# Causal attention feeding a soft mixture of experts: joining chunk maxima with two one-operand VectorE reductions on a gapped row, and routing products ahead of attention's value products

## Chip, cores and metric

One Trainium2 chip, one core. The metric is the device time of one execution in microseconds (us), and lower is better. The kernel before has a median of 550.02 us over three runs (547.91 to 552.44).

## What is computed

The reference, cut to what matters:

```python
def _attn_ref(q, k, v):                       # (8, 12, 448, 64) each, float32
    scores = scale * np.matmul(q, k.transpose(0, 1, 3, 2))
    scores = np.where(mask, -1000000000.0, scores)          # causal
    scores = scores - np.max(scores, axis=-1, keepdims=True)
    attn = np.exp(scores)
    attn = attn / (np.sum(attn, axis=-1, keepdims=True) + 1e-09)
    return np.matmul(attn, v)

def _moe_ref(x, phi, w1, w2):                 # x: (3584, 768), phi: (768, 32)
    logits = x @ phi
    d = softmax of logits over the 3584 tokens, per slot
    slot_out = 8 experts on d.T @ x           # 4 slots each, 768 -> 1024 -> 768, relu
    c = softmax of logits over the 32 slots, per token
    return c @ slot_out
```

Attention over 8 batches of 12 heads gives `x`, the input of a soft mixture of experts: every one of the 32 slots is a weighted sum of all tokens, goes through its expert, and is handed back to all tokens with other weights.

## The kernel before, in words

The engines are named as the profile does: PE (TensorE, with PEld for its weight loads), DVE (VectorE), ACT (ScalarE), POOL (GpSimd) and SP (SyncE, which issues the loads). Every operation is issued through a helper class that keeps each engine's instructions in the order in which the program writes them. So all instructions carry one line, L70, and groups are told apart by their tiles.

**The loop.** The 96 heads are taken one after the other (line 511), two heads to a pair that shares its loads. Twelve heads make a batch of the experts' part. One pass of the loop, number i, works on several heads at once, and the table `ORDER` (lines 48 to 53, one row for even passes and one for odd) says in which order it issues the steps:

- `c0`, `c3`, `c12`, `k0` to `k3`: the causal mask and the scores of head i+2 on PE, into tile `s`, 1024 columns of PSUM. Keys lie on the partitions in four chunks of 128, and chunk c has the columns of the queries that it may serve: 448, 320, 192 and 64 columns.
- `x0` to `x3` (`max_keys`, line 277): the largest score of each query block of head i+2, on DVE. `x0` is one transposing reduction of `s` into a row `r` of 32 numbers, one for each 32 columns of `s`. Since a query block lies in up to four chunks, `x1` to `x3` join the chunks: three `tensor_tensor` maxima, in place in `r`, of 10, 6 and 2 numbers.
- `mr0`, `mr1` (`max_row`): for head i+1, a PE transpose of 14 columns of `r` into `rt`, and a DVE reduction of it into `mr`.
- `sp` (`max_spread`): POOL spreads `mr` over the queries, into `r2`, for head i+1.
- `t0` to `t3` (`scores2`): PE adds the low-order parts of the operands and the maximum to the scores of head i.
- `exp`: ACT writes the exponentials of head i from `s` to `pt`.
- `a0` to `a3` (`attv`): PE multiplies `pt` of head i-1 with the values, 64 small products into `po`; `n0` to `n2` (`norm`): DVE adds epsilon to the sums (`sm`), takes the reciprocal, and writes the normalised head to `x`.
- `ck`, `cq`, `c2` on ACT (casts and copies of loaded keys and queries) and `sk`, `sq` on POOL (`tensor_tensor` subtractions, 64 x 896, that leave the low-order parts `ks` and `r2`): one of each for a pair.
- `pa` and `plan`: the experts' part. `pa` is a transpose of a finished pair (`xt` on PE, copied to `xts` by ACT), in passes 0, 1, 3, 5, 9 and 10 of each twelve, or a transpose of the weights (`tp`), in pass 4. `plan` is the products with the routing matrix (`g` on PE, added to `lt` by DVE; passes 2, 8 and 11, with two more small DVE steps, `bm` and `run_m`, in pass 2), or the slots' weighted sums (`sp` on PE, added to `si` by DVE; passes 6 and 7). Before the change `plan` is the last step of a pass, so on PE it stands behind the 64 value products and on DVE behind `n2`.

**Buffers that tie the engines.** `s` has three buffers. `rt`, `xt`, `tp`, `g` and the slots' sums share a single PSUM buffer (`misc`, line 210), so each of them waits until DVE or ACT has read the one before. `po` is single.

**After the loop** the expert weights that did not fit (23 of the tiles are loaded during the loop) stream in, the experts run on PE, and the result is written.

Of the kernel before, what the change touches and what calls it, by code (L numbers as in the profile page):

```python
# [9 lines left out]
F32 = mybir.dt.float32  # L10
# [3 lines left out]
ALU = mybir.AluOpType  # L14
AX = mybir.AxisListType
PSUM = bass.MemoryType.PSUM

P = 128
# [3 lines left out]
AW = 32  # L22
# [4 lines left out]
NQB = S // 32  # L27
# [4 lines left out]
NHD = 2 * NPAIR  # L32
# [14 lines left out]

ORDER = (
# [4 lines left out]
)  # L53

SC0, SC1, SC2, SC3 = 512, 0, 320, 960
CQ0 = (0, 128, 256, 384)
SCOL = (SC0, SC1, SC2, SC3)

# [27 lines left out]
def attention_soft_moe(ctx: ExitStack, tc: tile.TileContext, qk, va, phi, w1, w2, out):  # L86
    nc = _Core(tc)
# [7 lines left out]
    wk = early.enter_context(tc.tile_pool(name="wk", bufs=1, side="right"))  # L95
    fix = early.enter_context(tc.tile_pool(name="fix", bufs=1, side="right"))
# [6 lines left out]
    x_, va_, pt_ = [None] * XB, [None, None], [None, None]  # L103
    qd_, ks_ = ([fix.tile([P, 2, S], F32R, name=f"{o}0")] for o in ("qd", "ks"))
    x_[1] = fix.tile([P, NCH, 3 * P], F32, name="x1")
    qd_.append(fix.tile([P, 2, S], F32R, name="qd1"))
    zero = fix.tile([P, P // 2], F32, name="zero")
    ks_.append(fix.tile([P, 2, S], F32R, name="ks1"))
    r2_ = [fix.tile([P, 2, S], F32R, name="r20")]
    va_[0] = fix.tile([P, NCH, 2, VC], F32, name="va0")  # L110

    k2_ = fix.tile([P, 2, S], F32R, name="k2")
    r2_.append(fix.tile([P, 2, S], F32R, name="r21"))
    pt_[0] = wk.tile([P, 1025], F32, name="pt0")
    va_[1] = wk.tile([P, NCH, 2, VC], F32, name="va1")
    pt_[1] = wk.tile([P, 1025], F32, name="pt1")
    lt = moe.tile([P, P], F32, name="lt")

    x_[2] = moe.tile([P, NCH, 3 * P], F32, name="x2")
# [4 lines left out]
    st = {}  # L124
# [63 lines left out]
    ident = const.tile([P, P], F32, name="ident")  # L188
# [16 lines left out]
            nc.vector.memset(k2_[0:64, :, :].bitcast(F32), 1.0)  # L205
    nc.vector.memset(po0, 0.0)
    for i in range(2):
        nc.vector.memset(pt_[i][:, 1024:1025], 0.0)

    def misc(name):  # L210
        return ps_1.tile([P, 512], F32, tag="m", name=name)
# [64 lines left out]

    def max_keys(i, k):

        if i >= NHD:
            return  # L280
        if k == 0:
            r = st["r", i] = wk.tile([P, 32], F32, tag="r", name=f"r{i}", bufs=2)
            nc.vector.tensor_reduce(out=r, in_=st["s", i].rearrange("p (b k)->p b k", k=32),
                                    axis=AX.X, op=ALU.max, apply_transpose=True)
        else:
            r, c0, c, q = st["r", i], SC0 // 32, SCOL[k] // 32, CQ0[k] // 32
            rq = r[:, c0 + q:c0 + NQB]
            nc.vector.tensor_tensor(out=rq, in0=rq, in1=r[:, c:c + NQB - q], op=ALU.max)

    def max_row(i, k):  # L290
        if i >= NHD:
            return
        if k == 0:
            st["rt", i] = misc(f"rt{i}")
            nc.tensor.transpose(out=st["rt", i][0:NQB, 0:P], in_=st.pop(("r", i))[:, SC0 // 32:SC0 // 32 + NQB], identity=ident)
        else:
            mr = st["mr", i] = wk.tile([NQB, 32], F32, tag="mr", name=f"mr{i}", bufs=2)
            nc.vector.tensor_reduce(out=mr, in_=st.pop(("rt", i))[0:NQB, 0:P].rearrange("p (g t)->p t g", g=4),
                                    axis=AX.X, op=ALU.max, negate=True)

    def max_spread(i):
        if i >= NHD:
            return
        p, h = divmod(i, 2)
        mr = st.pop(("mr", i))

        nc.gpsimd.affine_select(out=r2_[p % NR][0:NQB, h].rearrange("p (b t)->p b t", t=32),
                                in_=mr.unsqueeze(1).to_broadcast([NQB, NQB, 32]),
                                compare_op=ALU.is_equal, fill=0.0, base=0,
                                pattern=[[-1, NQB], [0, 32]], channel_multiplier=1)  # L310
# [16 lines left out]
    def attv(i, qcs):  # L327
        if not 0 <= i < NHD:
            return
        p, h = divmod(i, 2)  # L330
        pt, v, po = pt_[i % 2], va_[p % 2], st.get(("po", i), po0)
        begun = st.setdefault(("begun", i, id(po)), set())
        for qc in qcs:
            for c in range(qc + 1):
                col = SCOL[c] + P * (qc - c)
                for u in range(0, P if qc < 3 or i == NHD - 1 and c < 3 else 64, AW):
                    nc.tensor.matmul(po[u:u + AW, qc], pt[:, col + u:col + u + AW], v[:, c, h],
                                     start=u not in begun, stop=c == qc, skip_group_check=True)
                    begun.add(u)
# [43 lines left out]
    def logits_b(b, l):  # L383
        bm = st["bm", b] = moe.tile([P, 1], F32, tag="bm", name=f"bm{b}", bufs=2)
        nc.vector.tensor_reduce(out=bm, in_=l, axis=AX.X, op=ALU.max, negate=True)

        mo, mn = run_m[(b + 1) % 2], run_m[b % 2]
        nc.vector.tensor_tensor(out=mn, in0=mo, in1=st.pop(("bm", b)), op=ALU.min)

    def logits_d(b, l):  # L390
        mo, mn = run_m[(b + 1) % 2], run_m[b % 2]
# [42 lines left out]
    plan, plan_a = {}, {}  # L434
    for b in range(NB):
        o, last = 12 * b, b == NB - 1
        for j, r in enumerate((3, 5, 9, 10, 12, 13)):
            if not last or j < PPB - 2:
                plan_a[o + r] = lambda p=b * PPB + j: xtrans(p)
        for j, r in ((0, 8), (2, 11)):  # L440
            plan[o + r] = lambda b=b, j=j: next_logits(b, j, misc(f"g{b}_{j}"))
        if not last:
            plan[o + 14] = lambda b=b: (next_logits(b, 4, misc(f"g{b}_4")), logits_b(b, lt))
            plan_a[o + 16] = lambda b=b: logits_e(b)
            plan[o + 18] = lambda b=b: dispatch(b, 0)
            plan[o + 19] = lambda b=b: dispatch(b, 1)
# [21 lines left out]
    copy_k2(0, h1)  # L468
    cast_q(1, h1)

    for i, k in ((0, 0), (0, 1), (0, 2), (0, 3), (1, 0)):
        max_keys(i, k)
    sub_k(1, h0)
    max_row(0, 0)
    warm(START[5], po0.rearrange("p a b->p (a b)")[:, 0:2 * P])
    scores1_all(2)
    warm(START[3])
    max_row(0, 1)
    max_spread(0)
    for k in (1, 2, 3):  # L480
        max_keys(1, k)
    sub_q(1, h0)

# [27 lines left out]
    for i in range(NHD):  # L511
        p, h = divmod(i, 2)
# [11 lines left out]
        if i < 2:  # L524
            scores2(i, (1, 0, 2))
            if i:
                scores1_all(3)
            scores2(i, (3,))
            exps(i)
            if i == 0:  # L530
                max_row(1, 0)
                warm(START[4], po0.rearrange("p a b->p (a b)")[:, 0:P])
                max_row(1, 1)
                sub_k(1, h1, nc.vector)
                max_spread(1)
                sub_q(1, h1)
# [37 lines left out]
    i, b, p = NHD - 1, NB - 1, NPAIR - 1  # L574
# [3 lines left out]
    mo, mn = run_m[(b + 1) % 2], run_m[b % 2]  # L578
# [5 lines left out]
    for k, qcs in ((2, (3, 2)), (4, (1, 0))):  # L584
        po = st["po", i] = ps[k][:, 0:NCH * VC].rearrange("p (c n) -> p c n", n=VC)
        attv(i, qcs)
        cs = slice(qcs[1], qcs[0] + 1)
        nc.vector.tensor_scalar(out=sm[:, cs], in0=po[:, cs, HD], scalar1=EPS, scalar2=None, op0=ALU.add)
        nc.vector.reciprocal(out=sm[:, cs], in_=sm[:, cs])
        nc.vector.tensor_tensor(out=x[:, cs, HD:2 * HD], in0=po[:, cs, 0:HD],  # L590
                                in1=sm[:, cs].unsqueeze(2).to_broadcast([P, 2, HD]), op=ALU.mult)
# [17 lines left out]
    for c in range(NCH):  # L609
# [11 lines left out]
                            axis=AX.X, op=ALU.min)  # L621
# [21 lines left out]
    for hf in range(2):  # L643
# [7 lines left out]
        else:  # L651
# [8 lines left out]
                            axis=AX.X, op=ALU.add)  # L660
# [4 lines left out]
    pt1 = pst.enter_context(tc.tile_pool(name="pt1", bufs=1, space=PSUM, reuse_waits="tile"))  # L665
# [218 lines left out]
```

## Time and profile before

The profiled execution took 551.62 us; its span, from the first to the last instruction, is 549.8 us. A pass of the loop is taken from one transpose into `rt` to the next.

| | before |
|---|---|
| median of three runs | 550.02 us |
| profiled execution, its span | 551.62 us, 549.8 us |
| DVE busy | 452.3 us (82%) |
| PE busy | 426.1 us (78%) |
| ACT busy | 288.4 us (52%) |
| POOL busy | 266.3 us (48%) |
| one pass of the loop, mean over 79 passes (80 reductions into `mr`, 62.8 to 429.5 us) | 4.64 us |
| first expert weights of the tail asked for | 438.0 us |

How to read it: the page gives busy time per engine and a span in 40 slices. The list of groups gives count, busy time and mean duration of all instructions of one kind. The timeline gives start and duration of each; in brackets stands the idle time of the engine before it and what ended that. The windows give busy time by stretch, with the granted share of PE's clock and of DMA time. Matmul ends are modelled.

### The profile page before, as it was taken

Reading aid. Unit: us, or ns where it says so; the run is one execution under the profiler, and the core shown is the slowest. Engines: PE = TensorE matmul, PEld = TensorE weight load, DVE = VectorE, ACT = ScalarE, POOL = GpSimd, SP = SyncE. Lnnn points to the kernel's source line nnn. Section 1 sums busy time; section 2 is a strip of 40 time slices with the busy share of each in tenths; the row PEclk is TensorE's granted clock in tenths of the full one; section 3 lists DMA queues with packets and bytes.
Section 4 is the critical chain, followed back from the end, with each engine's and each line's share of the span. In section 5 each row is a group of like instructions: output and inputs, shape, how many; then the busy total and the mean of one; then the engine's idle time right before and its main releaser. Section 6 shows DMA issues by size and latency. Waiting matters only on the chain.

```text
span 549.8 us, 20288 instructions
## 1 busy us (share of the span) xinstructions
PE 426.1 (78%) x8864; PEld 323.8 (59%) x8864; DVE 452.3 (82%) x954; ACT 288.4 (52%) x400; POOL 266.3 (48%) x216
## 2 busy tenths in 40 slices
PE   8676888777877787788787768777887699999870
PEld 4565667566656665676576557655766476454340
DVE  5999899899989999989999989998899955753360
ACT  5564657465746574656556646665565442133350
POOL 5776566555655565655566656665555510000000
PEclk9899888899989998988999999998888989999995
DMA  7366545455546455545545654555455589999998
GB/s 240 123 205 212 178 141 170 163 197 148 188 162 197 149 180 191 174 148 179 180 157 166 197 178 154 168 197 180 128 181 183 179 318 380 419 424 418 409 392 346
DMA packets 34504, 119.56 MB, mean 217 GB/s; under 512 B 3824, under 2 KB 8944, under 8 KB 32880
## 3 DMA queue, kind: packets, MB, share of 16 engines
q1 hardware_dynamic: 34272, 118.01, 61.5%
q8 instruction: 69, 1.13, 0.8%
q10 hardware_dynamic: 144, 0.27, 0.1%
q14 instruction: 19, 0.16, 0.1%
HBM read 107.25 MB, written 11.01 MB: 215 GB/s over the span
## 4 chain that ended last, share of the span: by engine, by line
DVE 65%; PE 15%; DMA 11%; issue 5%; ACT 1%; SPq 0%; DVEq 0%
DVE r L70 50%; DMA w<-in_w_dram 10%; PE po L70 5%; DVE sm L70 4%; DVE mr L70 4%; DVE x L70 4%; PE s L70 3%; PE rt L70 2%; DVE si L70 1%; PE xt L70 1%; PE pp L70 1%; PE e L70 1%; DMA qk<-in_qk_dram 1%; DVE lt L70 1%; PE hp L70 1%
## 5 line engine op out<-in xcount | busy, mean ns | idle before, releaser
L70 DVE TENSOR_TENSOR r<-r 128x10 f32<-128x10 f32 (+2 forms) x288 | 193.4, 671 | 9.8
L70 ACT ACTIVATE pt<-s 128x1024 f32<-128x1024 f32 x96 | 98.4, 1025 | 181.6 <-PE s L70 174.5
L70 POOL TENSOR_SCALAR_AFFINE_SELECT r<-mr 14x448 fp32r<-14x448 f32 x96 | 62.0, 645 | 170.6 <-DVE mr L70 156.4
L70 PE MATMUL po<-va,pt 128*32 128x65 f32 x6080 | 141.5, 235 | 1.0 <-issue 1.0
L70 PEld LDWEIGHTS po<-va,pt 128*32 128x32 f32 x6080 | 124.5, 118 | 15.7 <-issue 11.4
L70 DVE TRANSPOSE_TENSOR_REDUCE r<-s 128x32 f32<-128x1024 f32 x96 | 117.8, 1228 | 0.1
L70 POOL TENSOR_TENSOR r<-qk,qd 64x896 fp32r<-64x896 f32 (+1 forms) x50 | 101.1, 2023 | 7.2 <-ACT qd L70 3.4
L70 PE MATMUL rt<-ident,r 128*14 128x128 f32 x96 | 26.4, 275 | 95.8 <-DVE lt L70 31.4
L70 POOL TENSOR_TENSOR ks<-qk,ks 64x896 fp32r<-64x896 f32 (+1 forms) x47 | 97.6, 2076 | 3.8 <-ACT ks L70 0.2
L70 PE MATMUL s<-qd,ks 128*128 128x448 f32 (+3 forms) x384 | 80.4, 321 | 0.6 <-ACT qd L70 0.6
L70 PEld LDWEIGHTS rt<-ident,r 128*14 128x14 f32 x96 | 8.5, 89 | 114.6 <-DVE lt L70 36.3
L70 PE MATMUL s<-r,k 128*128 128x320 f32 (+3 forms) x384 | 70.9, 307 | 0.5 <-POOL r L70 0.5
L70 PEld LDWEIGHTS s<-qd,ks 128*128 128x128 f32 (+1 forms) x384 | 59.1, 192 | 2.2 <-ACT qd L70 1.5
L70 PEld LDWEIGHTS s<-r,k 128*128 128x128 f32 (+1 forms) x384 | 55.2, 179 | 2.6 <-POOL r L70 0.7
L70 ACT ACTIVATE ks<-qk 128x896 fp32r<-128x896 f32 (+1 forms) x50 | 45.6, 914 | 4.4 <-DMA qk<-in_qk_dram 3.2
L70 ACT ACTIVATE k<-ks 64x896 fp32r<-64x896 f32 (+1 forms) x49 | 45.8, 934 | 1.2
L70 ACT ACTIVATE qd<-qk 128x896 fp32r<-128x896 f32 (+1 forms) x50 | 45.9, 918 | 0.6 <-DMA qk<-in_qk_dram 0.5
L70 DVE TENSOR_TENSOR x<-po,sm 128x256 f32<-128x256 f32 x95 | 40.3, 424 | 3.3
L70 PE MATMUL s<-tri,identb 128*128 128x64 bf16 (+2 forms) x288 | 42.7, 246 | 0.0
L70 DVE TENSOR_REDUCE mr<-rt 14x32 f32<-14x128 f32 x96 | 26.3, 274 | 17.9 <-PE rt L70 17.5
L70 PEld LDWEIGHTS <-identb 128*128 128x128 bf16 x339 | 25.0, 100 | 24.0 <-issue 18.7
L70 PE MATMUL xt<-ident,x 128*128 128x128 f32 x188 | 32.3, 297 | 1.8 <-DVE mr L70 0.5
(135 smaller groups left out, 374.8 us busy)
## 6 DMA issues: line engine op xcount, KB each, us to landing
qk<-in_qk_dram SPq DMA_DIRECT2D x94, 448.0 KB, 3.4
w<-in_w_dram SPq DMA_DIRECT2D x43, 768.0 KB, 5.9
w<-in_w_dram SPq DMA_DIRECT2D x10, 1536.0 KB, 19.5
va<-in_va_dram SPq DMA_DIRECT2D x47, 260.0 KB, 2.7
out_dram<-ot SPq DMA_DIRECT2D x16, 384.0 KB, 6.7
out_dram<-ot SPq DMA_DIRECT2D x2, 1536.0 KB, 9.5
qk<-in_qk_dram SPq DMA_DIRECT2D x4, 224.0 KB, 3.6
hw<-in_w_dram SPq DMA_DIRECT2D x1, 768.0 KB, 5.5
```

The source lines that it names most:

```text
L70: return self._tc.keep_in_program_order(op(*args, **kwargs))
```

## The change

Two things change, and a few that follow from them.

1. **Joining of the maxima.** `x1` to `x3` (three `tensor_tensor` instructions with two operands, both in `r`) become `x1` and `x2`, two `tensor_reduce` instructions with one operand. For this the columns of `s` are laid out anew (chunk 0 from column 576, chunk 3 from 512), `r` becomes one of two fixed tiles of 96 columns, filled once with -3.0e38, and `x0` writes its 32 numbers in two runs of 16, 36 columns apart. Read with the right strides, the row then holds the chunks of one query block beside each other: `x1` reduces pairs (32 numbers to 16), `x2` reduces triples (18 numbers to 6) for the last six blocks. The running minimum `run_m`, once a batch, becomes a `tensor_scalar` as well.
2. **Order.** `plan` moves from the end of a pass to the place right behind `x0`: on PE ahead of the 64 value products, on DVE ahead of `x1`, `x2` and the normalisation.

With the new layout the last head needs 2 extra value products in place of 6, and `pt` has 1024 columns in place of 1025.

```diff
-     "x0", "x1", "x2", "x3", "cq", "a0", "a1", "a2", "a3", "n0", "n1", "n2", "ld", "plan"),
+     "x0", "plan", "x1", "x2", "cq", "a0", "a1", "a2", "a3", "n0", "n1", "n2", "ld"),
...
-     "x0", "x1", "x2", "x3", "a0", "a1", "a2", "a3", "n0", "n1", "n2", "ld", "plan"),
+     "x0", "plan", "x1", "x2", "a0", "a1", "a2", "a3", "n0", "n1", "n2", "ld"),
...
-SC0, SC1, SC2, SC3 = 512, 0, 320, 960
+SC0, SC1, SC2, SC3 = 576, 0, 320, 512
+RW, RC, RF = 96, 4, 20
...
+    r_ = [fix.tile([P, RW], F32, name=f"r{i}") for i in range(2)]
...
-        nc.vector.memset(pt_[i][:, 1024:1025], 0.0)
+        nc.vector.memset(r_[i], -3.0e38)
...
+        r = r_[i % 2]
         if k == 0:
-            r = st["r", i] = wk.tile([P, 32], F32, tag="r", name=f"r{i}", bufs=2)
-            nc.vector.tensor_reduce(out=r, in_=st["s", i].rearrange("p (b k)->p b k", k=32),
+            nc.vector.tensor_reduce(out=r[:, RC:RC + 72].rearrange("p (a b)->p a b", b=36)[:, :, 0:16],
+                                    in_=st["s", i].rearrange("p (a b k)->p a b k", a=2, k=32),
                                     axis=AX.X, op=ALU.max, apply_transpose=True)
+        elif k == 1:
+            w = r[:, 0:84].rearrange("p (j q)->p q j", j=2)[:, 0:16]
+            nc.vector.tensor_reduce(out=r[:, RF:RF + 76].rearrange("p (a q)->p a q", a=2)[:, :, 0:8],
+                                    in_=w.rearrange("p (a q) j->p a q j", a=2), axis=AX.X, op=ALU.max)
         else:
-            r, c0, c, q = st["r", i], SC0 // 32, SCOL[k] // 32, CQ0[k] // 32
-            rq = r[:, c0 + q:c0 + NQB]
-            nc.vector.tensor_tensor(out=rq, in0=rq, in1=r[:, c:c + NQB - q], op=ALU.max)
+            nc.vector.tensor_reduce(out=r[:, RF + 8:RF + NQB],
+                                    in_=r[:, 14:80].rearrange("p (j q)->p q j", j=3)[:, 0:6],
+                                    axis=AX.X, op=ALU.max)
...
-                for u in range(0, P if qc < 3 or i == NHD - 1 and c < 3 else 64, AW):
+                for u in range(0, P if qc < 3 or i == NHD - 1 and c == 3 else 64, AW):
...
-        nc.vector.tensor_tensor(out=mn, in0=mo, in1=st.pop(("bm", b)), op=ALU.min)
+        nc.vector.tensor_scalar(out=mn, in0=mo, scalar1=st.pop(("bm", b))[:, 0:1], scalar2=None, op0=ALU.min)
...
-    for i, k in ((0, 0), (0, 1), (0, 2), (0, 3), (1, 0)):
+    for i, k in ((0, 0), (0, 1), (0, 2), (1, 0)):
```

What moves on DVE, in pass 2 of the second batch (`r` is the row of maxima, `po` the value products, `g` the routing products, `lt` their running sum). Before:

```order
L70 TENSOR_REDUCE r_2082<-s_2063 128x32
L70 TENSOR_TENSOR r_2082<-r_2082 128x10
L70 TENSOR_TENSOR r_2082<-r_2082 128x6
L70 TENSOR_TENSOR r_2082<-r_2082 128x2
L70 TENSOR_SCALAR sm_2120<-po 128x4
L70 RECIPROCAL sm_2120<-sm_2120 128x4
L70 TENSOR_TENSOR x_87<-po,sm_2120 128x4x64
L70 TENSOR_TENSOR lt<-g_4_2124,lt 128x128
L70 TENSOR_REDUCE bm_2134<-lt 128x1
L70 TENSOR_TENSOR run_m_230<-run_m_229,bm_2134 128x1
L70 TENSOR_REDUCE mr_2154<-rt_2152 14x32
```

and in the changed program:

```order
L71 TENSOR_REDUCE r_90<-s_2009 128x2x16
L71 TENSOR_TENSOR lt<-g_4_2029,lt 128x128
L71 TENSOR_REDUCE bm_2039<-lt 128x1
L71 TENSOR_SCALAR run_m_228<-run_m_227,bm_2039 128x1
L71 TENSOR_REDUCE r_90<-r_90 128x2x8
L71 TENSOR_REDUCE r_90<-r_90 128x6
L71 TENSOR_SCALAR sm_2077<-po 128x4
L71 RECIPROCAL sm_2077<-sm_2077 128x4
L71 TENSOR_TENSOR x_87<-po,sm_2077 128x4x64
L71 TENSOR_REDUCE mr_2098<-rt_2096 14x32
```

The three steps of the routing sum, which frees the shared PSUM buffer, stand right behind the transposing reduction now, and the row `r` is read and written by reductions of one operand.

On PE, in the same pass, from the transpose into `rt` on. Before:

```order
L70 MATMUL rt_2071<-ident,r_2021 14x128
L70 MATMUL s_1921<-r_94,k_93 128x448
L70 MATMUL s_1921<-r_94,k_93 128x192
L70 MATMUL s_1921<-r_94,k_93 128x320
L70 MATMUL s_1921<-r_94,k_93 64x64
L70 MATMUL po<-va_92,pt_97 32x65 x32
L70 MATMUL g_4_2124<-xts_1945,phi_226 32x128 x4
L70 MATMUL g_4_2124<-xts_2019,phi_226 32x128 x4
```

and in the changed program:

```order
L71 MATMUL rt_2017<-ident,r_91 14x128
L71 MATMUL s_1871<-r_96,k_95 128x448
L71 MATMUL s_1871<-r_96,k_95 128x320
L71 MATMUL s_1871<-r_96,k_95 128x192
L71 MATMUL s_1871<-r_96,k_95 64x64
L71 MATMUL g_4_2029<-xts_1895,phi_224 32x128 x4
L71 MATMUL g_4_2029<-xts_1967,phi_224 32x128 x4
L71 MATMUL po<-va_94,pt_99 32x65 x32
```

The routing products have changed places with the value products. ACT, POOL and SP issue the same instructions in the same order as before.

More of the change, by code (lines that the diff above doesn't have):

```diff
@@ L113, in attention_soft_moe @@
     r2_.append(fix.tile([P, 2, S], F32R, name="r21"))
-    pt_[0] = wk.tile([P, 1025], F32, name="pt0")
+    pt_[0] = wk.tile([P, 1024], F32, name="pt0")
     va_[1] = wk.tile([P, NCH, 2, VC], F32, name="va1")
-    pt_[1] = wk.tile([P, 1025], F32, name="pt1")
+    pt_[1] = wk.tile([P, 1024], F32, name="pt1")
     lt = moe.tile([P, P], F32, name="lt")
@@ L294, in max_row @@
             st["rt", i] = misc(f"rt{i}")
-            nc.tensor.transpose(out=st["rt", i][0:NQB, 0:P], in_=st.pop(("r", i))[:, SC0 // 32:SC0 // 32 + NQB], identity=ident)
+            nc.tensor.transpose(out=st["rt", i][0:NQB, 0:P], in_=r_[i % 2][:, RF:RF + NQB], identity=ident)
         else:
@@ L479, in attention_soft_moe @@
     max_spread(0)
-    for k in (1, 2, 3):
+    for k in (1, 2):
         max_keys(1, k)
```

## Prediction

> **What bounds the kernel now.** I read the page first (busy time by engine), then the windows (which stretch is which), then the groups of DVE, and then the timeline of single passes, because only there can it be seen who waits for whom.
>
> ```profile
> PE 426.1 (78%) x8864; PEld 323.8 (59%) x8864; DVE 452.3 (82%) x954; ACT 288.4 (52%) x400; POOL 266.3 (48%) x216
> DVE r L70 50%; DMA w<-in_w_dram 10%; PE po L70 5%; DVE sm L70 4%; DVE mr L70 4%; DVE x L70 4%; PE s L70 3%; PE rt L70 2%; DVE si L70 1%; PE xt L70 1%; PE pp L70 1%; PE e L70 1%; DMA qk<-in_qk_dram 1%; DVE lt L70 1%; PE hp L70 1%
> 40.00:430.00 390.00, 303.19 (x7022) 246.16 (x7025) 360.17 (x722) 230.00 (x295) 231.69 (x176) 0.94 0.53 172
> 445.00:549.80 104.80, 81.55 (x1138) 47.02 (x1136) 47.49 (x145) 30.59 (x72) 1.48 (x3) 0.93 0.98 388
> L70 DVE TENSOR_REDUCE mr<-rt x80: 268/274/281, 62.8 to 429.5; 14x32 f32<-14x128 f32 x80
> 438.00 0.80 SPq L70 DMA_DIRECT2D w<-in_w_dram  x2
> ```
>
> The second row is the chain of waits: half of it is DVE's work on `r`. The two windows (span, then PE, PEld, DVE, ACT, POOL busy, PE's granted clock, DMA share, GB/s) split the program: in the loop DVE is busy 360.17 of 390 us, 92%; in the tail DMA is busy 98% of the time. The reduction into `mr` comes once a pass: (429.5 - 62.8) / 79 = 4.64 us a pass. The tail begins when its weights are asked for at 438.0 us, and from there it is DMA's; nothing in the change touches that. So the question is what a pass costs, for the 90 or so passes before 438 us (near pass 91; the first, at 5 to 20 us, wait for loads).
>
> The groups of DVE by form (count | busy us, mean ns), and two of POOL:
>
> ```profile
> L70 DVE TENSOR_TENSOR r<-r 128x10 f32<-128x10 f32 x96 | 158.8, 1654 | 3.3
> L70 DVE TRANSPOSE_TENSOR_REDUCE r<-s 128x32 f32<-128x1024 f32 x96 | 117.8, 1228 | 0.1
> L70 DVE TENSOR_TENSOR r<-r 128x6 f32<-128x6 f32 x96 | 17.8, 185 | 3.3
> L70 DVE TENSOR_TENSOR r<-r 128x2 f32<-128x2 f32 x96 | 16.8, 175 | 3.3
> L70 DVE TENSOR_REDUCE emask<-sid 128x8 f32<-128x32 f32 x1 | 0.2, 176 | 0.0
> L70 POOL TENSOR_TENSOR r<-qk,qd 64x896 fp32r<-64x896 f32 x46 | 96.6, 2100 | 3.7
> L70 POOL TENSOR_SCALAR_AFFINE_SELECT r<-mr 14x448 fp32r<-14x448 f32 x96 | 62.0, 645 | 170.6 <-DVE mr L70 156.4 <-PE s L70 12.6 <-DVE r L70 1.5
> ```
>
> Ten numbers a partition take 1654 ns where six take 185. The timeline shows what the first one does:
>
> ```profile
> 309.98 2.10 POOL L70 TENSOR_TENSOR ks<-qk,ks 64x896 fp32r<-64x896 f32 x1
> 310.38 1.73 DVE L70 TENSOR_TENSOR r<-r 128x10 f32<-128x10 f32 x1
> 446.27 0.57 DVE L70 TENSOR_TENSOR r<-r 128x10 f32<-128x10 f32 x3
> ```
>
> The DVE instruction ends at 312.11, POOL's subtraction at 312.08. It is not computing, it waits until POOL is done. At 446.27, after POOL's last subtraction, all three together take 0.57 us. In the loop the same three take 2.12 us (below): 1.55 us of each pass is this wait, counted as busy. The Trainium skill (SBUF — State Buffer, section Who interferes with whom) has the rule: a DVE instruction with two SBUF inputs contends with a GpSimd instruction that reads SBUF, and on trn2 a `tensor_reduce` never does. The trace agrees with its first half by these rows; its second half is this forecast.
>
> One whole pass with a transposition, and the start of the next:
>
> ```profile
> 304.28 0.28 PE L70 MATMUL rt<-ident,r 128*14 128x128 f32 x1 [1.84 <-DVE lt L70]
> 304.31 0.71 PE L70 MATMUL s<-r,k 128*128 128x448 f32 x4
> 304.66 0.28 DVE L70 TENSOR_REDUCE mr<-rt 14x32 f32<-14x128 f32 x1
> 304.87 1.23 DVE L70 TRANSPOSE_TENSOR_REDUCE r<-s 128x32 f32<-128x1024 f32 x1
> 305.01 0.64 POOL L70 TENSOR_SCALAR_AFFINE_SELECT r<-mr 14x448 fp32r<-14x448 f32 x1 [2.16 <-DVE mr L70]
> 305.58 1.33 PE L70 MATMUL po<-va,pt 128*32 128x65 f32 x64
> 305.74 2.10 POOL L70 TENSOR_TENSOR r<-qk,qd 64x896 fp32r<-64x896 f32 x1
> 306.13 2.13 DVE L70 TENSOR_TENSOR r<-r 128x10 f32<-128x10 f32 x3
> 307.01 0.69 PE L70 MATMUL s<-qd,ks 128*128 128x320 f32 x3
> 307.09 0.60 ACT L70 ACTIVATE xts<-xt 128x512 f32<-128x512 f32 x1
> 308.18 0.15 DVE L70 TENSOR_SCALAR sm<-po 128x4 f32<-128x4 f32 x1
> 308.36 0.18 DVE L70 RECIPROCAL sm<-sm 128x4 f32<-128x4 f32 x1
> 308.40 0.27 PE L70 MATMUL rt<-ident,r 128*14 128x128 f32 x1 [0.71 <-DVE sm L70]
> 308.58 0.42 DVE L70 TENSOR_TENSOR x<-po,sm 128x256 f32<-128x256 f32 x1
> 308.92 0.27 DVE L70 TENSOR_REDUCE mr<-rt 14x32 f32<-14x128 f32 x1
> ```
>
> PE works without a pause from 304.28 to 307.70 (3.42 us), then stands 0.70 us: the next `rt` needs the last of the three maxima, which ends at 308.26 by its row (the row's merged time; the transpose starts as it closes). So there is a ring: `mr`, POOL's spreading, POOL's subtraction, the three maxima behind it, the normalisation, `mr`: 4.12 us.
>
> A pass with routing products is worse:
>
> ```profile
> 243.17 0.27 PE L70 MATMUL rt<-ident,r 128*14 128x128 f32 x1 [0.70 <-DVE sm L70]
> 245.02 0.60 PE L70 MATMUL g<-xts,phi 128*32 128x128 f32 x14
> 245.14 2.12 DVE L70 TENSOR_TENSOR r<-r 128x10 f32<-128x10 f32 x3
> 245.73 0.69 PE L70 MATMUL s<-qd,ks 128*128 128x448 f32 x3
> 247.92 0.28 DVE L70 TENSOR_TENSOR lt<-g,lt 128x128 f32<-128x128 f32 x1
> 248.26 0.28 PE L70 MATMUL rt<-ident,r 128*14 128x128 f32 x1 [1.84 <-DVE lt L70]
> ```
>
> PE is done after 243.17 to 246.42 (3.25 us) and stands 1.84 us, because `rt` uses the PSUM buffer that `lt` has yet to read, and `lt` is DVE's last step: 5.09 us.
>
> **The change, part by part.**
>
> *The joins.* Three `tensor_tensor` instructions go, 1654 + 185 + 175 = 2.01 us. Two reductions of 32 and 18 numbers come. Their price is not in the trace for this use; the nearest row is the reduction of 32 numbers within SBUF, 176 ns (no POOL work ran then). From below: 2 x 0.18 = 0.36 us. From above: each waits for POOL as the first maximum did, and the pair costs 2.01 - 0.18 = 1.83 us. I take 0.40: the reduction `mr` and the transposing one run in the loop at their usual time though POOL's subtraction starts under the latter (304.87 to 306.10 against 305.74). These read PSUM, so this speaks for it without proving it.
>
> *The other DVE steps.* Starts to starts: `mr` 0.21, transposing reduction 1.26, two joins 0.40, `sm` 0.18, reciprocal 0.22, `x` 0.34: 2.61 us a pass; with `lt`, and in pass 2 the two small steps (0.32 each), up to 3.4. The gapped output of the first reduction has no row: from below no change, from above one more run at 1.23; I take none. DVE is then no longer the longest engine.
>
> *Where the stall goes.* POOL has 0.65 + 2.10 = 2.75 us a pass, ACT 230.0 / 390 x 4.64 = 2.74, so both fit under PE. PE's own work is what is late next: 3.42 us with a transposition (at whose end ACT's `xts` is also just done: 307.69, so `rt` finds its buffer free), 3.25 with routing products; for the slots' sums and pass 2 I put 3.5 and 3.4. Over twelve passes: (6 x 3.45 + 3 x 3.3 + 3.3 + 2 x 3.5) / 12 = 3.41 us.
>
> *The move of `plan`.* On PE the 0.6 us of `g` now stand ahead of the 64 value products. `g` needs the shared buffer, that is `mr`, which ends 0.66 us after `rt` starts (304.28 to 304.94), while PE is busy with `rt` and the second scores until 305.02: no wait. The value products end later by 0.6 us, and with them the normalisation behind; it has 3.41 - 2.61 = 0.8 us to spare. In return `lt` runs about 2 us after `rt`, and the 1.84 us stall of the five passes is gone. If DVE were still held up in the joins, `lt` would still be ahead of them, so the move has a gain of its own.
>
> *The smaller edits.* The `run_m` instruction (seven times), the fills of two tiles at the start under the first loads, and four small products less at the end: nothing.
>
> *The half clock.* PE's granted clock is 0.94 in the loop; some passes run partly slower. A PE without the long pauses should lose less of this. I count no gain beyond using full-clock passes for the 3.41.
>
> *Sum.* 3.41 is a floor with every wait hidden. ACT has passes with 0.86 us of extra exponentials, DVE and PE come within 0.1 us of each other in pass 2, and jitter in so tight a ring costs: I add 0.14 (between 0 and 0.44, which would be the 3.85 of the second rival), 3.55 us a pass. 90 x (4.64 - 3.55) = 98 us. 551.6 - 98 = 453.6; the median of the runs is 1.6 us under the profiled run. I predict **454 us**. With the floor itself, 551.6 - 90 x 1.23 = 441.
>
> **Rivals.**
>
> *A: another DVE step takes over the wait for POOL.* In the loop of before no `sm`, reciprocal or `x` ever ran beside a subtraction, since the first maximum stood in front. Now they will start 2.8 us after `rt`, while POOL's subtraction runs from about 1.5 to 3.6 us. If `sm` or the reciprocal is held, the ring is POOL's end, `sm`, reciprocal, `x`, `mr`, spreading, subtraction: 4.24 us today (305.74 to 309.98) less the two later maxima and their gaps, 0.3: 3.93; 551.6 - 90 x 0.71 = 488. Against it: `sm` reads PSUM. For it: the reciprocal goes from SBUF to SBUF. The Trainium skill (VectorE: DVE Perf Modes, What auto-detection actually checks) says that a single-source instruction with source and destination in SBUF may be run through both ports, and names conditions the 128x4 reciprocal would meet; no row here shows one beside POOL. Chance 0.14.
>
> *B: PE does not pack.* Its busy time in the loop is 303.19 / 390 x 4.64 = 3.61 us a pass. If that is its true need, at 0.94 of the clock, and a quarter of a microsecond of waits stays: 3.85; 551.6 - 90 x 0.79 = 480. Against it: the pauseless 3.42 and 3.25 above. Chance 0.15.
>
> *C: the change does not do what it says.* If any DVE instruction that reads SBUF waits for POOL's subtraction, the reductions cost 1.83 us. Only the move helps: transposition passes 3.95, the others 4.1 in place of 5.1, together 4.05; 551.6 - 90 x 0.59 = 498. Chance 0.04.
>
> *D: slower.* The transposing reduction, with an output in two runs of 16 and strided reads behind it, could be slow in itself. Transposing reduction and joins are 1.23 + 2.01 = 3.24 us today; only from a transposing reduction of 2.9 us on is the new set dearer. At three times its time, 3.7 us, a pass has 2.61 + 2.45 + 0.3 = 5.3 us on DVE: 551.6 + 90 x 0.7 = 615. Nothing in the rows speaks for it, except that no gapped output is there to see. Chance 0.03.
>
> **How the numbers follow.** The forecast (441 to 470) has 0.64, A 0.14, B 0.15, C 0.04, D 0.03. The range is 440 to 492: the floor below, A above; it leaves out C, D and a little of A. A measurement of this kernel can tell about 1% from no change. All cases but D are faster by more than that: faster 0.96, within 1% 0.01, slower 0.03.
>
> **What would show each step right or wrong.** Right: the group of the first join drops from 158.8 us to about 20 and the second is like it; DVE's share in the loop falls from 92% to about 75%; PE's rises over 90% and its clock towards 1.0; `rt` no longer waits for `lt` or `si`; passes with and without `plan` differ by under 0.3 us; the tail still takes about 112 us from its first weights. A shows as a long `sm`, reciprocal or `x` that ends with a POOL subtraction; B as PE busy 95% with passes of 3.8 us; C as joins of 1.5 us; D as a longer transposing reduction. The forecast is wrong if passes stay over 3.9 us.

## The result, and the profile after

The changed kernel takes 434.27 us (median; 432.75 to 442.69) beside 549.22 us for the kernel before: a ratio of 0.7891, 95% interval 0.7839 to 0.7943. Ratios here are formed without runs over 1.5% above the fastest of their kernel: the run of 442.69 us, and the longest one each of experiments 4 and 10. The forecast was 454 us, 440 to 492: the right direction and, in the main, the right mechanism, but the gain is 115 us where 95 were forecast, and the time lies under the range.

The execution profiled with this result took 442.69 us, 8 us over the median; where places are compared below, a second profile of the same kernel, from a later measurement (437.38 us, 435.96 to 439.23), stands beside it. The page and the loop's window of the first:

```profile
span 441.0 us, 20205 instructions
PE 399.9 (91%) x8856; PEld 312.9 (71%) x8856; DVE 301.9 (68%) x858; ACT 288.2 (65%) x400; POOL 266.6 (60%) x216
PEclk9999999999999998999999999999999899999985
DMA 10%; PE 6%; DVE 3%; ACT 1%; issue 1%; SPq 0%
40.00:320.00 280.00, 269.56 (x6808) 228.67 (x6796) 217.44 (x619) 223.08 (x288) 225.59 (x167) 0.99 0.72 234
```

DVE's busy time is down by 150 us, PE is busy 96% of the loop at 0.99 of its clock, and DVE 78%. `r` is gone from the chain of waits, where it had 50%. This chain could not be followed back through the whole loop, so its shares are small. That of the second profile reaches further back, and PE has the largest share:

```profile
PE 41%; DMA 10%; issue 2%; ACT 1%; DVE 1%; ACTq 0%
```

The tail is as long as forecast: from the asking for its first weights to the end it takes 111.8 us before (438.0 to 549.8) and 112.5 in the second profile (325.0 to 437.5).

DVE's groups in the first profile:

```profile
L71 DVE TRANSPOSE_TENSOR_REDUCE r<-s 128x32 f32<-128x1024 f32 x96 | 117.8, 1227 | 0.1
L71 DVE TENSOR_REDUCE r<-r 128x16 f32<-128x32 f32 x96 | 17.2, 179 | 2.0
L71 DVE TENSOR_REDUCE r<-r 128x6 f32<-128x18 f32 x96 | 16.8, 175 | 3.3
L71 DVE TENSOR_SCALAR sm<-po 128x4 f32<-128x4 f32 x95 | 15.4, 162 | 45.7 <-PE po L71 44.2
L71 DVE RECIPROCAL sm<-sm 128x4 f32<-128x4 f32 x95 | 16.9, 178 | 3.2
L71 DVE TENSOR_TENSOR x<-po,sm 128x256 f32<-128x256 f32 x95 | 40.3, 425 | 3.3
```

The joins take 0.35 us in place of 2.01, and the transposing reduction with its gapped output costs what it did (1227 against 1228 ns). `sm` now waits 44.2 us for the value products: DVE waits for PE, not PE for DVE.

A pass with a transposition, one with routing products, and the start of the next (timeline; start, duration):

```profile
95.23 0.27 PE L71 MATMUL rt<-ident,r 128*14 128x128 f32 x1
95.97 0.64 POOL L71 TENSOR_SCALAR_AFFINE_SELECT r<-mr 14x448 fp32r<-14x448 f32 x1 [0.43 <-PE s L71]
96.69 2.10 POOL L71 TENSOR_TENSOR r<-qk,qd 64x896 fp32r<-64x896 f32 x1
97.08 0.40 DVE L71 TENSOR_REDUCE r<-r 128x16 f32<-128x32 f32 x2
97.91 0.16 DVE L71 TENSOR_SCALAR sm<-po 128x4 f32<-128x4 f32 x1 [0.43 <-PE po L71]
98.03 0.60 ACT L71 ACTIVATE xts<-xt 128x512 f32<-128x512 f32 x1
98.10 0.18 DVE L71 RECIPROCAL sm<-sm 128x4 f32<-128x4 f32 x1
98.32 0.42 DVE L71 TENSOR_TENSOR x<-po,sm 128x256 f32<-128x256 f32 x1
98.68 0.28 PE L71 MATMUL rt<-ident,r 128*14 128x128 f32 x1
99.40 0.65 PE L71 MATMUL g<-xts,phi 128*32 128x128 f32 x16
100.44 0.24 DVE L71 TENSOR_TENSOR lt<-g,lt 128x128 f32<-128x128 f32 x1
101.79 0.27 PE L71 MATMUL rt<-ident,r 128*14 128x128 f32 x1
```

Both joins together take 0.40 us while POOL's subtraction (96.69 to 98.79) goes on, and `sm`, the reciprocal and `x` run beside it at their usual times. The first pass is 3.45 us, and its end is set by `xts`, which leaves the shared PSUM buffer at 98.63, 0.05 us ahead of `rt`. The second is 3.11 us; `lt` is done 1.1 us before the next `rt`.

From the starts of `rt`, medians by kind of pass in us, from 40 us on (the kernels below the change are those of the experiments):

| kernel | transposition, even | transposition, odd | routing products | weights' transpose | slots' sums |
|---|---|---|---|---|---|
| before | 4.25 | 4.24 | 5.09 | 4.25 | 5.36 |
| the change (both profiles within 0.01) | 3.26 | 3.46 | 3.11 | 3.11 | 3.32 |
| joins only | 3.26 | 3.46 | 3.25 | 3.11 | 3.57 |
| order only | 4.25 | 4.25 | 4.25 | 4.25 | 4.25 |
| one two-operand instruction more | 3.85 | 3.85 | 3.85 | 3.85 | 3.85 |
| three one-operand instructions more | 3.27 | 3.45 | 3.34 | 3.11 | 3.41 |
| POOL writes only | 3.26 | 3.46 | 3.41 | 3.11 | 3.74 |
| `xts` ahead of the keys' copy | 3.26 | 3.26 | 3.11 | 3.20 | 3.32 |
| products 64 wide | 3.31 | 3.46 | 3.30 | 3.16 | 3.51 |
| both edits | 3.31 | 3.31 | 3.30 | 3.16 | 3.52 |
| diagonal products only | 2.75 | 3.46 | 2.65 | 2.99 | 2.84 |

### The profile page after: what moved, and what is told of

Same layout as the page of the kernel before. It is cut to its first block, busy times and chain, and to the rows that moved or that the text cites. A ratio compares the mean times of both kernels' runs of the same rounds, so it can differ in the third digit from the quotient of the medians.

```text
span 441.0 us, 20205 instructions
## 1 busy us (share of the span) xinstructions
PE 399.9 (91%) x8856; PEld 312.9 (71%) x8856; DVE 301.9 (68%) x858; ACT 288.2 (65%) x400; POOL 266.6 (60%) x216
## 5 line engine op out<-in xcount | busy, mean ns | idle before, releaser
L71 PE MATMUL po<-va,pt 128*32 128x65 f32 x6080 | 129.6, 221 | 10.9 <-issue 10.7
L71 PEld LDWEIGHTS po<-va,pt 128*32 128x32 f32 x6080 | 115.7, 109 | 28.5 <-issue 27.5
L71 DVE TRANSPOSE_TENSOR_REDUCE r<-s 128x32 f32<-128x1024 f32 x96 | 117.8, 1227 | 0.1
L71 PE MATMUL s<-qd,ks 128*128 128x448 f32 (+3 forms) x384 | 77.3, 312 | 0.9 <-POOL ks L71 0.7
L71 PEld LDWEIGHTS s<-qd,ks 128*128 128x128 f32 (+1 forms) x384 | 55.7, 182 | 3.0 <-POOL ks L71 1.2
L71 DVE TENSOR_SCALAR sm<-po 128x4 f32<-128x4 f32 x95 | 15.4, 162 | 45.7 <-PE po L71 44.2
L71 PE MATMUL s<-tri,identb 128*128 128x64 bf16 (+2 forms) x288 | 40.9, 238 | 0.1
L71 DVE TENSOR_REDUCE r<-r 128x16 f32<-128x32 f32 x192 | 34.0, 177 | 5.3
L71 PE MATMUL xt<-ident,x 128*128 128x128 f32 x188 | 31.3, 290 | 0.5 <-issue 0.5
L71 ACT ACTIVATE xts<-xt 128x512 f32<-128x512 f32 x47 | 28.0, 596 | 1.2 <-PE xt L71 0.5
```

Source lines behind the costliest of these rows:

```text
L71: return self._tc.keep_in_program_order(op(*args, **kwargs))
```

## The experiments

The theory: a DVE instruction with two operands in SBUF waits for POOL's subtraction; that closed the ring (a chain of waits that comes back to its start one pass later) that set a pass, and with it gone PE's own work sets it. The first rival: the gain comes from the order of `plan`, or from fewer small instructions.

**1. Joins only.** `plan` goes back to the end of a pass, in the row of even passes shown and in the odd one alike.

```diff
-     "x0", "plan", "x1", "x2", "cq", "a0", "a1", "a2", "a3", "n0", "n1", "n2", "ld"),
+     "x0", "x1", "x2", "cq", "a0", "a1", "a2", "a3", "n0", "n1", "n2", "ld", "plan"),
```

> The joins as two one-operand reductions, but plan at the end of a pass as before. Theory (the wait for POOL's subtraction was the loop's ring, and PE is the bound now): nearly the whole gain, passes with plan about 0.2 to 0.3 us longer than in the changed kernel because lt and si stand behind the normalisation, so 440 to 448 us. Rival (the order of plan did most of it): about 510 us.

Measured: 440.16 us, ratio 0.7997 (0.7965 to 0.8029). The joins alone bring nearly everything. Passes with `plan` are 0.14 and 0.25 us longer, near the 0.2 to 0.3 that were expected; three at 0.14 and two at 0.25 make 0.08 us a pass over twelve, 7 us in all. The medians of the changed kernel are 3 and 6 us lower (the second profile's measurement and the first), and the intervals of the ratio overlap with the former (0.7914 to 0.7973 there). In the profiles the loop is not longer without the move: from the first reduction into `mr` to the last it takes 321.7 us with the joins only, and 326.3 and 323.8 us in the two profiles of the change, because pauses of PE, seen under experiment 7, take the 7 us back. So what the move is worth beside the joins is not settled by these runs.

**2. Order only.** The kernel before with `plan` moved, in both rows alike.

```diff
-     "x0", "x1", "x2", "x3", "cq", "a0", "a1", "a2", "a3", "n0", "n1", "n2", "ld", "plan"),
+     "x0", "plan", "x1", "x2", "x3", "cq", "a0", "a1", "a2", "a3", "n0", "n1", "n2", "ld"),
```

> Plan right behind x0, but the three two-operand maxima and the old layout as before. Theory: passes with a transposition keep 4.13 to 4.25 us, passes with plan fall from about 5.1 to about 4.2 us, so 505 to 515 us. Rival (the order did most of it): under 460 us.

Measured: 518.07 us, ratio 0.9402 (0.9367 to 0.9438). That is 3 us over the expected range. Every kind of pass is 4.25 us now: `plan` hides under the wait, and the ring through POOL stays. The group says that the wait is still there:

```profile
L70 DVE TENSOR_TENSOR r<-r 128x10 f32<-128x10 f32 x96 | 141.4, 1473 | 2.0
```

The two parts are not additive: 33 us by the order alone, 111 by the joins alone, 115 with both. With the ring in place the order takes 0.84 and 1.11 us off the passes with `plan` (5.09 and 5.36 to 4.25); with the ring gone, 0.14 and 0.25.

**3. One two-operand instruction put back.**

```diff
+            rq = r[:, RF + 8:RF + NQB]
+            nc.vector.tensor_tensor(out=rq, in0=rq, in1=rq, op=ALU.max)
```

> The changed kernel with one more DVE instruction in each pass behind the second join: a tensor_tensor maximum of 6 numbers with themselves, both operands in SBUF; the result is the same. Theory (any two-operand instruction on SBUF waits until POOL's subtraction ends): it takes about 1.3 us instead of 0.2, the ring through POOL comes back at about 3.9 us a pass, 475 to 490 us. Rival (the number and size of the small instructions was what cost): 0.2 us more on DVE, at most 0.2 us a pass, under 455 us.

Measured: 484.52 us, ratio 0.8798 (0.8764 to 0.8832). In its timeline and groups:

```profile
200.81 2.08 POOL L71 TENSOR_TENSOR ks<-qk,ks 64x896 fp32r<-64x896 f32 x1
201.64 1.28 DVE L71 TENSOR_TENSOR r<-r 128x6 f32<-128x6 f32 x1
202.92 0.16 DVE L71 TENSOR_SCALAR sm<-po 128x4 f32<-128x4 f32 x1
203.50 0.27 PE L71 MATMUL rt<-ident,r 128*14 128x128 f32 x1
L71 DVE TENSOR_TENSOR r<-r 128x6 f32<-128x6 f32 x96 | 111.6, 1162 | 3.3
```

Six numbers take 1162 ns, because the instruction ends with POOL (202.92 against 202.89). All passes are 3.85 us, the ring of the forecast's rival A (3.93) to 0.08.

**4. Three one-operand instructions put in at the same place.**

```diff
+            rq = r[:, RF + 8:RF + NQB]
+            for _ in range(3):
+                nc.vector.tensor_reduce(out=rq, in_=rq.unsqueeze(2), axis=AX.X, op=ALU.max)
```

> The changed kernel with three more one-operand reductions of 6 numbers in each pass behind the second join; the result is the same. Theory: 0.6 us more on DVE, none of them waits for POOL, and DVE has that much to spare beside PE in most passes: 434 to 446 us, so less than one two-operand instruction costs. Rival (the number of small instructions was what cost): 0.6 us a pass, about 490 us.

Measured: 442.49 us (438.75 to 446.43), ratio 0.7993 (0.7938 to 0.8048). Three cost 5 to 8 us; one with two operands cost 47 to 50.

```profile
L71 DVE TENSOR_REDUCE r<-r 128x6 f32<-128x6 f32 x288 | 45.9, 159 | 10.0
```

So neither count nor size of the small instructions matters, but the second operand. And it matters where it comes from, not that the instruction is a `TENSOR_TENSOR`: in the changed kernel's first profile `lt` and `x`, which read one operand from PSUM and one from SBUF, start while a subtraction runs in 14 and 73 cases and take 240 and 425 ns on average, where they took 279 and 424 before. DVE had most of this 0.5 us to spare; pass 2, where it has the most to do, got longer (3.6 us).

**5. The change unaltered, on the chip of the next three.**

> The changed kernel unaltered, beside the next two on the same chip: 432 to 436 us, and a profile whose passes are 3.25 (even, with a transposition), 3.45 (odd, with a transposition), 3.1 (routing products, weights) and 3.3 us (slots' sums), mean under 3.4.

Measured: 437.38 us, ratio 0.7944 (0.7914 to 0.7973), 1.4 us over the expectation. The kinds of pass came out as expected, but their mean, from `mr`, is (333.5 - 9.7) / 95 = 3.41 us, over the 3.29 that the ordinary passes of a batch give: a few passes hold a pause of PE, seen under experiment 7.

**6. `xts` ahead of the keys' copy.** In odd passes ACT copies the transposed pair before it copies the keys.

```diff
-    ("c3", "c0", "k3", "c12", "k0", "k1", "k2", "mr0", "mr1", "sp", "t0", "t1", "t2", "t3", "sq", "exp", "c2", "pa",
-     "x0", "plan", "x1", "x2", "a0", "a1", "a2", "a3", "n0", "n1", "n2", "ld"),
+    ("c3", "c0", "k3", "c12", "k0", "k1", "k2", "mr0", "mr1", "sp", "t0", "t1", "t2", "t3", "sq", "exp", "pa",
+     "c2", "x0", "plan", "x1", "x2", "a0", "a1", "a2", "a3", "n0", "n1", "n2", "ld"),
```

> The changed kernel, with ACT's copy of the transposed pair (xts) ahead of its copy of the keys (k) in odd passes. Theory (odd passes with a transposition are 3.45 us, not 3.25, because the next rt waits until xts has freed the shared PSUM buffer): four passes of twelve fall by 0.2 us, 30 of them, so 426 to 430 us. Rival (PE's own work sets those passes too): within 1 us of the changed kernel. A loss would say that the second scores then wait for k.

Measured: 438.56 us (436.26 to 440.33), ratio 0.7966 (0.7934 to 0.7997). The time did not fall, where 426 to 430 us were expected. The passes that it aims at did, from 3.46 to 3.26 us, as the theory has it, and `rt` no longer waits for `xts`: this row of the second profile of the change has none like it here.

```profile
PEld rt L71 <- ACT xts L71: 7.4, 22, 1.0
```

In the profiles the loop is 2.4 us shorter (321.4 beside 323.8 us, first `mr` to last); the weights' transpose got 0.09 longer, and passes with a pause or another delay took more than in the change (the sums stand under experiment 7). Inconclusive by itself, which led to experiment 8.

**7. Products 64 queries wide.**

```diff
-AW = 32
+AW = 64
```

> The changed kernel with the value products 64 queries wide in place of 32: half as many products and weight loads, each on twice the columns of the array. If the pauses of PE that wait for nothing the profile shows come with the number of its instructions, they become rarer and the time falls by 2 to 8 us; if PE's time for these products goes by columns moved one group after the other, a pass gets longer by up to 0.5 us, up to 480 us.

Measured: 433.05 us (432.41 to 434.23), ratio 0.787 (0.7841 to 0.7899), on the same chip as 437.38. Ordinary passes got longer by up to 0.2 us, and the time still fell by 1%; the two kernels' ranges do not meet (435.96 to 439.23 there), though the first measurement of the change, from 432.75 us on, does meet it. The value products of the changed kernel (second profile) at one place, and the rows of the instruction queue and of the waits that nothing in the profile explains:

```profile
163.80 0.99 PE L71 MATMUL po<-va,pt 128*32 128x65 f32 x52
166.96 0.54 PE L71 MATMUL po<-va,pt 128*32 128x65 f32 x12 [2.17 <-issue]
q8 instruction: 69, 1.13, 1.0%
PEld po L71 <- issue: 27.4, 96, 2.3
```

and those of the wider products:

```profile
q8 instruction: 45, 0.74, 0.7%
PEld po L71 <- issue: 22.5, 90, 0.6
```

In the changed kernel PE stops in the middle of 64 products for 2.17 us, with nothing that it waits for in the profile. In the two profiles of the changed kernel 13 such pauses of over 0.6 us lie between 20 and 320 us, and each ends 1.29 to 1.48 us after a 16 KB packet of queue 8, of instructions, has landed. With half as many products there are 45 of these packets in place of 69, and no such pause.

What the pauses and the delays around them cost can be summed: of 82 passes (about 50 us to the end of the loop), those that lie over 0.1 us above the median of their kind hold 13.4 and 12.5 us of excess in the two profiles of the change, 14.8 in experiment 6, and nothing with the wider products or with both edits.

That PE waits for its instructions is the reading that fits the constant distance and the going away together; no run shows it directly. The number of packets does not decide by itself: the kernel with the joins only has 69 packets too, and there one such pause (1.02 us) and 3.9 us of excess. Why some packets come late and most do not is open (the loads of data share the DMA engines, which carry 234 GB/s in the loop in place of 172).

**8. Both edits.**

> The changed kernel with both edits: the value products 64 queries wide, and ACT's copy of the transposed pair ahead of its copy of the keys in odd passes. Theory (with the pauses of PE's instruction supply gone, the 0.2 us that odd passes wait for the shared PSUM buffer show in the time): odd passes 3.3 instead of 3.45, 4 to 6 us under the wider products alone, so 427 to 431 us, and better than the changed kernel. Rival (PE's own work is the floor of every pass): as the wider products alone, 432 to 434 us.

Measured: 429.01 us (428.84 to 430.82), ratio 0.7795 (0.7771 to 0.7819), faster than the changed kernel (0.7944 and 0.7891) and than experiment 7 (0.787). With the pauses gone, the 0.15 us of the odd passes show (3.46 to 3.31). This is the fastest kernel that computes everything.

**9. Writes in place of subtractions.** In the kernel before, POOL fills the rows in place of subtracting into them, in all pairs but the first two; the low-order parts of keys and queries are left out. Shown for `ks`; the rows of `r2` get the same.

```diff
+            if hs.stop - hs.start == 2:
+                for _ in range(2):
+                    nc.gpsimd.memset(ks.bitcast(F32), 0.0)
+                return
```

> The kernel before, with POOL's two subtractions of a pair replaced by two fills each (0.84 us each, 1.68 us together, against 2.10), in all pairs but the first two: POOL then writes the same rows but reads nothing, and the low-order parts of keys and queries are left out. Theory (the two-operand maxima wait for POOL instructions that read SBUF): the first maximum falls from 1654 to about 200 ns and the time to 455 us or less. Rival (any POOL instruction on SBUF holds it): the first maximum still takes 1.2 us, about 510 us.

Measured: 450.8 us, ratio 0.8198 (0.8166 to 0.8229).

```profile
L70 DVE TENSOR_TENSOR r<-r 128x10 f32<-128x10 f32 x96 | 16.6, 173 | 3.3
L70 POOL MEMSET r<- 64x896 f32 x94 | 79.0, 841 | 5.2
```

With three two-operand maxima, the old order, and POOL busy for 1.68 us at the same place, the first maximum takes 173 ns; in 87 of its 96 runs it starts while a fill goes on. So it is POOL's reading that holds it. The rule of the Trainium skill (SBUF — State Buffer, Who interferes with whom) says just this, that an instruction which only writes is not in the way, and the trace agrees.

**10. Diagonal products only.** The attention of a query to the keys of earlier chunks is left out, which takes value products off PE.

```diff
-            for c in range(qc + 1):
+            for c in range(qc if i < NHD - 1 else 0, qc + 1):
```

> The changed kernel with the value products of the diagonal blocks alone in all heads but the last: 14 of 32 products remain, the attention of a query to keys of earlier chunks is left out. This takes about 0.7 us of PE work from each pass. Theory (PE's work sets a pass now): passes fall until POOL's 2.75 and ACT's up to 3.5 us stop them, to 2.8 to 3.1 us, so 385 to 410 us. Rival (a ring through ACT, POOL and DVE sets it): less than 10 us gained.

Measured: 407.99 us (405.08 to 413.75), ratio 0.7394 (0.735 to 0.7438).

```profile
40.00:290.00 250.00, 217.41 (x3833) 172.37 (x3833) 206.73 (x610) 219.93 (x285) 223.14 (x166) 0.99 0.79 258
PEld rt L71 <- ACT xts L71: 29.2, 31, 1.7
```

With less PE work, even passes with a transposition and those with routing products fall by 0.5 us, so PE's work did set these. The odd ones stay at 3.46: there `rt` waits for ACT's `xts`. PE is at 87% in the window and POOL at 89%.

## Why the forecast was right, and why it was too high

- *What bounded the kernel* (the ring through POOL's subtraction, the second ring through `lt`): right, by experiments 2, 3 and 9. In the profile of before, 93 of the 96 first maxima start while a subtraction runs, and each of these ends within 60 ns of its end.
- *The joins* at 0.40 us: right (0.40 from the first's start to the second's end). *The gapped output* at no price: right.
- *The move of `plan`*: right that nothing waits for it and that `lt` leaves the ring. Its gain beside the joins is 7 us by the ordinary passes and not clear in the time (experiment 1).
- *Rival A* did not come. The reciprocal starts while a subtraction runs in 76 of 95 cases of the first profile and takes 178 ns as before, so the rule of the Trainium skill on running a single-source instruction through both ports (VectorE: DVE Perf Modes, What auto-detection actually checks), whose conditions its operands would meet, does not reach it here.
- *Rival B* did not come: PE packs, to 96% busy.
- *The half clock*: counted at nothing beyond full-clock passes; the clock is 0.99 or 1.00.
- *The floor of 3.41 us a pass* is the step that failed, together with the number of passes (below). The ordinary passes are 3.26, 3.46, 3.11, 3.11 and 3.32; over twelve, (2 x 3.26 + 4 x 3.46 + 3 x 3.11 + 3.11 + 2 x 3.32) / 12 = 3.29. I had measured PE's work from the start of `rt` to the end of the last score product. That end is modelled, and the next `rt` starts before it:

```profile
162.18 0.69 PE L71 MATMUL s<-qd,ks 128*128 128x448 f32 x3
162.70 0.27 PE L71 MATMUL rt<-ident,r 128*14 128x128 f32 x1
```

  The product ends at 162.87 by its row, and `rt` starts at 162.70. The overlap is 0.16 to 0.17 us in every kind of pass that PE ends, eight of twelve, and was counted twice: 0.11 us a pass on average, nearly the whole difference. The odd passes with a transposition came out at the 3.45 that was put for them, but by luck: the forecast took that for PE's own work, with the buffer free for `rt`, and they end with `xts` (experiments 6 and 8). Neither the 3.4 us for pass 2 nor the 3.5 for the slots' sums had a row behind it; measured in the forecast's way they are 3.27 and 3.48, so the former was too long. DVE's "up to 3.4" us in pass 2 was too much as well, for that pass takes 3.11.
- *The 0.14 us for waits*: of the right size by accident. The profiled means are 3.41 and 3.43 over the 3.29 of ordinary passes, but the waits are PE's pauses (experiment 7), not the ones that I named. So the sum's 3.55 us a pass was too high by the 0.12 of the floor.
- *90 passes* was the other term. From the first `mr` to the last:

```profile
L70 DVE TENSOR_REDUCE mr<-rt x96: 235/274/281, 11.6 to 448.3; 14x32 f32<-14x128 f32 x96
L71 DVE TENSOR_REDUCE mr<-rt x96: 236/279/280, 9.7 to 333.5; 14x32 f32<-14x128 f32 x96
```

  (before, and the second profile). All 95 intervals shrank, 436.7 to 323.8 us: 112.9 us where I had 98. The work before the first `mr` gave 1.9, and the tail behind the last one took 2.5 more (101.5 to 104.0). Spans: 549.8 to 437.5, which is 112.3. Against the forecast's 98, the five passes make 5 us, and 0.10 us more saved a pass makes the other 10 (3.41 in place of 3.55 after, less 4.60 in place of 4.64 before). This account goes from one profiled execution to another, 551.62 to 439.23 us. The median of the result lies 5 us under the latter; no profile of so fast a run is there, so where these 5 us go is not shown.
- *The range* ended at 440, which was that floor with those 90 passes. A floor made of modelled ends is no lower bound, and neither is a count of passes that falls short.
- *The signs*: the joins' groups, DVE's share, PE's share and clock, the waits of `rt` for `lt` and `si` and the tail came as named. Passes with and without `plan` differ by up to 0.35 us (3.46 and 3.11) where under 0.3 was named, again by the odd passes and their `xts`.

## What to carry to other kernels

A tiny instruction with a long mean duration is a wait in disguise: look at what ends together with it. Here a 10-number maximum waited for the other engine that reads SBUF, and the cure was to phrase it with one operand by laying out the row, which costs nothing, while one two-operand instruction left in would have given back some 50 us. When the ring is gone, the next bound is to be measured from start to start of an engine's instructions, and one should ask what the old slack was hiding: here pauses of PE that look like its instruction supply.

## What the runs showed of the hardware that was not expected

Pauses of PE, 0.6 to 2.4 us each, that end 1.29 to 1.48 us after a 16 KB instruction packet landed (13 of 13 in two profiles); they cost more than wider, in themselves slower, products (up to 0.2 us a pass). In these few runs the times also spread less without them: 432.41 to 434.23 and 428.84 to 430.82 us, beside 435.96 to 439.23.
